# Decay matrix, plain casts and a new order of work in the opening of a fused retention and gated feed-forward kernel

## The chip, the core and the metric

The kernel runs on one core of a Trainium2 chip. The metric is the device time of one launch in microseconds (us), lower is better. It is given as the median of several runs. The profile shows one such execution.

[...] DMAs in this kernel are issued by SP and by POOL, and a few by ACT. All of them move data with the same 16 DMA engines. Each engine works through its own instructions in the order in which the program wrote them, and waits on semaphores for the others.

## The reference: what is computed

A recurrent attention with one decay per head (4 batches, 8 heads, 768 steps, head size 64) feeds a feed-forward block with a cosine gate (model size 512, inner size 2048).

```python
gamma = 1.0 - 2.0 ** (-5.0 - np.arange(H))
scale = 1.0 / np.sqrt(D)
for t in range(S):
    state = gamma[None, :, None, None] * state + np.einsum('bhd,bhe->bhde', k[:, :, t], v[:, :, t])
    y[:, :, t] = scale * np.einsum('bhd,bhde->bhe', q[:, :, t], state)
x = y.transpose(0, 2, 1, 3).reshape(B * S, H * D)
h = x @ w_in
out = (h * np.cos(h)) @ w_out
```

Inputs and outputs are float32. The kernel multiplies in bf16.

## The kernel before

**Tiles.** The 768 steps are cut into 6 chunks of 128. Two batches are handled together, so there are 12 "pairs" p = 0 to 11: chunk p mod 6 of batches 2·(p div 6) and the next one. The letter b (0 or 1) is the batch within the pair. A load of q, k or v for one pair and one b is a DMA of 256 KB. Two pairs make a group g of 512 tokens, for which the feed-forward part runs.

**The decay.** The factor gamma^(i-j) between step i and step j is split: q is multiplied by scale·gamma^i (table `gq`) and v by gamma^-j (table `gk`), so that the product of both gives the decay. The tables are made from `pos`, which POOL counts out (`iota`, L133), by eight small multiplications on DVE (L142) and two exponentials on ACT (L144, L145). The score matrix then needs only a mask of ones and zeros (`mask`).

**Stages of a pair.** `conv_q` (L156) and `conv_v` (L161) multiply by the tables and convert to bf16, `conv_k` (L166) only converts. `stage_t` (L173) transposes q and k on PE, eight small transposes for each b, and copies the PSUM bank out to `qkt` with ACT or DVE (L184, L186); from pair 4 on DMA transposes do this (`stage_t_dma`, L189). `stage_a` (L202) forms the scores of one b in two banks, one for each half j of the heads. `stage_m` (L214) multiplies each bank by the mask into `am`, on DVE. `stage_y` (L222) forms the output of both b from `am`, v and the state of the pairs before, copies it to `xt` on ACT (L240), then adds the pair's k and v to the state in PSUM (L248) and copies the state to `stb` (L253). `attend` is `stage_a` and `stage_m` for both b.

**The feed-forward part.** `pair_f` (L275) and `unit_f` (L267) multiply `xt` by `w_in` (L282, L270); `act` takes the cosine on ACT (L261) and the product on DVE (L265) into `gt`. `unit_o` (L291) multiplies `gt` by `w_out` (L296).

**What sets the order.** The order is written out by hand (`manual_schedule`), instruction by instruction, for all engines. PSUM banks are taken from and given back to a first-in first-out list of seven. `warm(n)` (L316) issues n matmuls on zeros, whose result is not used. The opening is the code from L325 to L355. In it the POOL queue holds loads of pair 0 and 1, the four `w_in` loads, `conv_v(1)`, three `w_out` loads and the loads of pairs 2 and 3; the SP queue holds five loads (L130, L131). After that the loop works through groups with the same stages in between.

Of the kernel before, what the change touches and what calls it, by code (L numbers as in the profile page):

```python
# [30 lines left out]
def kernel(  # L31
# [11 lines left out]
    C = 128  # L43
# [31 lines left out]
    sb([128, 1], FP32, "pad")  # L75
# [24 lines left out]
    gk = sb([128, NC, H], FP32, "gk")  # L100

# [29 lines left out]
    load(nc.sync, 1, ("q0", "v0"))  # L131
    load(nc.gpsimd, 0, ("k1",))
    nc.gpsimd.iota(pos, pattern=[[C, NC]], base=1, channel_multiplier=1,  # L133
                   allow_small_or_imprecise_dtypes=True)
    load(nc.gpsimd, 0, ("v0", "v1"))
    make_identity(nc, ident)
# [3 lines left out]
    nc.vector.memset(mask, 1.0)  # L140
    for h in range(H):
        nc.vector.tensor_scalar(out=lgp[:, :, h], in0=pos, scalar1=float(lg[h]),  # L142
                                scalar2=None, op0=ALU.mult)
# [3 lines left out]
    for t in stb:  # L147
        nc.vector.memset(t, 0.0)
    nc.gpsimd.affine_select(out=mask, in_=mask, compare_op=ALU.is_ge, fill=0.0,
                            base=0, pattern=[[1, 128]], channel_multiplier=-1)  # L150
# [5 lines left out]
    def conv_q(p, eng):  # L156
        for b in range(2):
            eng.tensor_tensor(out=qs[p % NB][:, b], in0=qf[SLOT[p]][b],  # L158
                              in1=bc(gq, p % NC), op=ALU.mult)
# [13 lines left out]
    def stage_t(p, split, fill=0):  # L173
        n = p % NB
        for b in range(2):
            if fill:
                warm(fill * b)
            bank = banks.take()
            tr = bank.bitcast(BF16).rearrange("p (w a t) -> p w a t", w=2, a=HP)
            for w, src in enumerate((qs[n], ks[n])):  # L180
                for a in range(HP):
                    nc.tensor.transpose(tr[:, w, a, :], src[:, b, 2 * a : 2 * a + 2, :], ident)  # L182
            if split is None or split and b == 1:
                nc.vector.tensor_copy(out=qkt[n][:, :, b], in_=tr)  # L184
            else:
                nc.scalar.copy(out=qkt[n][:, :, b], in_=tr)  # L186
            banks.give(bank)
# [26 lines left out]
    def stage_m(p, item):  # L214
        b, bk, ap = item
        for j in range(2):
            nc.vector.tensor_tensor(  # L217
                out=am[p % 2][b][j], in0=ap[j],
                in1=mask.unsqueeze(1).to_broadcast([128, HP, 128]), op=ALU.mult)
            banks.give(bk[j])  # L220

    def stage_y(p, copy_st=nc.vector.tensor_copy):  # L222
        c = p % NC
        n = p % NB
        for b in range(2):
            bank = banks.take()
            yp = bank.rearrange("p (a t) -> p a t", a=HP)
            for a in range(HP):
                if c > 0:
                    for j in range(2):  # L230
                        nc.tensor.matmul(  # L231
                            yp[ts(j, 64), a, :], lhsT=stb[p % 2][:, b, a, ts(j, 64)],
                            rhs=qt(n, b, a), start=True, stop=False,
                            skip_group_check=True)
                for j in range(2):
                    nc.tensor.matmul(  # L236
                        yp[ts(j, 64), a, :], lhsT=vs[n][:, b, 2 * a + j, :],
                        rhs=am[p % 2][b][j][:, a, :], start=(c == 0), stop=True,
                        skip_group_check=True)
            nc.scalar.copy(out=xt[(p // 2) % 2][:, :, ts(2 * (p % 2) + b, C)], in_=yp)  # L240
            banks.give(bank)
        if c == NC - 1:
            return
        for b in range(2):
            for a in range(HP):
                for j in range(2):
                    h = 2 * a + j
                    nc.tensor.matmul(  # L248
                        st_ps[ts(j, 64), b, a, :], lhsT=ks[n][:, b, h, :],
                        rhs=vs[n][:, b, h, :], start=(c == 0 and b == 0 and a == 0),  # L250
                        stop=True, skip_group_check=True)
        for j in range(2):
            copy_st(out=stb[(p + 1) % 2][ts(j, 64), :, :, ts(j, 64)], in_=st_ps[ts(j, 64)])  # L253

# [70 lines left out]
    load(nc.gpsimd, 1, ("k0", "q1", "k1", "v1"))  # L325
    for r in range(4):
        load_w_in(r)
    conv_v(1, nc.gpsimd)
    for r in range(3):
        load_w_out(r)  # L330
# [6 lines left out]
    conv_q(0, nc.vector)  # L337
    conv_k(0, True)
    conv_v(0, nc.vector)
    stage_t(0, False)  # L340
    warm(3)
    attend(0)
    conv_k(1, True)
    conv_q(1, nc.vector)
    warm(6)
    stage_y(0, nc.scalar.copy)
    warm(2)
    stage_t(1, None)
    attend(1)
    banks.give(spare)  # L350
    pair_f(0, 0, (0,))
    stage_y(1, nc.scalar.copy)
# [7 lines left out]
    for part in range(3):  # L360
        for j in range(4):
            unit_o(0, j, part)
            if part == 2 and j == 0:
                stage_t(2, None)
                conv_v(2, nc.vector)
            elif part == 2 and j == 1:
                stage_m(2, stage_a(2, 0))
            elif part == 2 and j == 3:
                stage_m(2, stage_a(2, 1))
# [12 lines left out]
    stage_t(3, None)  # L382
# [100 lines left out]
```

## Time and profile before

| | |
|---|---|
| median of 6 runs | 212.51 us (212.02 to 213.2) |
| time of the profiled execution | 212.39 us |
| its span, first to last instruction | 210.6 us |
| PE busy | 201.5 us, 96% |
| DVE, ACT, POOL busy | 116.1, 113.4, 84.3 us |
| first matmul of `w_in` (L282) | 16.68 us |
| second group of them, after the state of pair 1 (L282, 24 matmuls) | 19.48 us |
| HBM read, written | 27.26 MB, 6.29 MB |

The profiled execution spends 1.8 us outside its span. Times in a timeline count from the start of the span. A line of a timeline has a start, a duration, the engine, the source line, the operation, the tile written and the tiles read, and how many instructions are merged into it; in brackets stands how long the engine was idle before it and what it was waiting for. A line of the chain of waits has a start, a duration and the engine or DMA that the work passed through. In the view by stretches each row gives a start and an end, the length, and the busy time of every engine.

### The profile page before, as it was taken

How to read it: one execution, taken by the hardware profiler on the slowest of the kernel's cores; microseconds unless marked ns; L12 is line 12 of the kernel's file. 1: busy time of each engine (PE TensorE's matmuls, PEld its weight loads, DVE VectorE, ACT ScalarE, POOL GpSimd, SP SyncE). 2: the span in 40 equal slices, each digit the busy share in tenths (PEclk: the TensorE clock that was granted, in tenths of full speed). 3: DMA queues.
4: the chain of work that ended last, by engine and by line, in shares of the span. 5: the costliest groups of instructions: out<-in, count | busy, mean ns of one | idle time of the engine just before them, and what ended most of it. 6: DMA issues, size and time to landing. Idle time of an engine off the chain costs nothing.

```text
span 210.6 us, 4148 instructions
## 1 busy us (share of the span) xinstructions
PE 201.5 (96%) x1637; PEld 112.6 (53%) x1637; DVE 116.1 (55%) x187; ACT 113.4 (54%) x183; POOL 84.3 (40%) x98
## 2 busy tenths in 40 slices
PE   7678999999999999999999999999999999999992
PEld 2347654548998554555455455445545444444440
DVE  5496776281976755859585385484482333343000
ACT  5665884228799336656835745745545554553110
POOL 7995238499977907999352400000000000000000
PEclk9999999999999999999999999999999999999999
DMA  6999999999999999989998321321101101110121
GB/s 160 327 248 207 220 253 290 336 258 313 216 228 227 201 306 273 240 240 271 274 172 202 91 61 50 88 66 50 50 3 50 50 3 50 50 50 26 75 91 61
DMA packets 55844, 33.83 MB, mean 161 GB/s; under 512 B 47248, under 2 KB 49552, under 8 KB 55824
## 3 DMA queue, kind: packets, MB, share of 16 engines
q1 hardware_dynamic: 49472, 17.70, 36.9%
q0 software_dynamic: 6208, 15.73, 28.4%
q8 instruction: 13, 0.21, 0.4%
q10 hardware_dynamic: 144, 0.13, 0.2%
q14 instruction: 7, 0.06, 0.1%
HBM read 27.26 MB, written 6.29 MB: 159 GB/s over the span
## 4 chain that ended last, share of the span: by engine, by line
PE 88%; DVE 5%; DMA 3%; issue 1%; POOL 1%; ACT 0%; POOLq 0%; DVEq 0%
PE bank L296 39%; PE bank L270 32%; PE bank L282 8%; DMA vf<-in_v_dram 3%; PE bank L209 3%; PE bank L231 3%; PE bank L236 2%; DVE am L217 2%; DVE qs L158 1%; PE st_ps L248 1%; PE bank L182 1%; DVE qkt L184 1%; DVE vs L163 1%; POOL kf L112 0%; POOL vf L112 0%
## 5 line engine op out<-in xcount | busy, mean ns | idle before, releaser
L265 DVE TENSOR_TENSOR gt<-bank,cosb 128x512 bf16<-128x512 f32 x96 | 65.6, 690 | 63.5 <-ACT cosb L261 63.0
L261 ACT ACTIVATE cosb<-bank,halfpi 128x512 bf16<-128x512 f32 x96 | 65.5, 687 | 53.2 <-PE bank L270 46.8
L296 PE MATMUL bank<-w_out_sb,gt 128*128 128x512 bf16 x384 | 93.3, 379 | 0.0
L270 PE MATMUL bank<-xt,w_in 128*128 128x512 bf16 x304 | 75.1, 380 | 0.0
L296 PEld LDWEIGHTS <-gt 128*128 128x128 bf16 x384 | 36.7, 98 | 42.7
L270 PEld LDWEIGHTS <-w_in 128*128 128x128 bf16 x304 | 33.8, 114 | 30.8 <-issue 0.2
L217 DVE TENSOR_TENSOR am<-bank,mask 128x512 bf16<-128x512 f32 x48 | 30.2, 681 | 0.0
L158 POOL TENSOR_TENSOR qs<-qf,gq 128x512 bf16<-128x512 f32 x18 | 18.6, 1048 | 20.9 <-DMA qf<-in_q_dram 15.0
L308 ACT COPY ob<-bank 128x512 f32<-128x512 f32 x23 | 13.4, 587 | 23.0 <-PE bank L296 22.9
L112 POOL DMA_DIRECT2D kf<-in_k_dram x23 | 20.8, 907 | 4.5 <-DMA w_out_sb<-in_moe_w_out_dram 2.1
L163 POOL TENSOR_TENSOR vs<-vf,gk 128x512 bf16<-128x512 f32 x20 | 20.7, 1052 | 1.1 <-DMA vf<-in_v_dram 1.0
L282 PE MATMUL bank<-xt,w_in 128*128 128x256 bf16 x160 | 18.6, 273 | 0.0
L169 ACT CAST ks<-kf 128x512 bf16<-128x512 f32 x24 | 13.8, 614 | 8.3 <-DMA kf<-in_k_dram 8.3
L282 PEld LDWEIGHTS <-w_in 128*128 128x128 bf16 x160 | 17.1, 114 | 0.5
L112 POOL DMA_DIRECT2D vf<-in_v_dram x16 | 14.2, 889 | 4.2 <-DMA w_out_sb<-in_moe_w_out_dram 4.2
L240 ACT CAST xt<-bank 128x512 bf16<-128x512 f32 x24 | 13.0, 587 | 3.3 <-DVE gt L265 3.0
L236 PE MATMUL bank<-am,vs 128*64 128x128 bf16 x192 | 12.1, 219 | 0.9 <-DVE am L217 0.9
L236 PEld LDWEIGHTS <-vs 128*64 128x64 bf16 x192 | 10.1, 110 | 1.7 <-issue 1.7
L231 PEld LDWEIGHTS <-stb 128*64 128x64 bf16 x160 | 8.7, 109 | 4.3 <-issue 3.8
L231 PE MATMUL bank<-qkt,stb 128*64 128x128 bf16 x160 | 10.6, 222 | 0.0
L253 DVE CAST stb<-st_ps 64x512 bf16<-64x512 f32 x12 | 8.2, 687 | 3.5 <-PE st_ps L248 3.3
L209 PE MATMUL bank<-qkt 64*128 64x128 bf16 x192 | 8.2, 218 | 0.7 <-DVE qkt L184 0.4
(38 smaller groups left out, 70.0 us busy)
## 6 DMA issues: line engine op xcount, KB each, us to landing
kf<-in_k_dram POOLq DMA_DIRECT2D x23, 256.0 KB, 6.1
out_dram<-ob SPq DMA_DIRECT2D x23, 256.0 KB, 2.2
qf<-in_q_dram SPq DMA_DIRECT2D x19, 256.0 KB, 6.3
vf<-in_v_dram POOLq DMA_DIRECT2D x16, 256.0 KB, 6.7
vf<-in_v_dram SPq DMA_DIRECT2D x8, 256.0 KB, 5.8
w_in<-in_moe_w_in_dram POOLq DMA_DIRECT2D x4, 512.0 KB, 10.3
w_out_sb<-in_moe_w_out_dram POOLq DMA_DIRECT2D x4, 512.0 KB, 13.4
qf<-in_q_dram POOLq DMA_DIRECT2D x5, 256.0 KB, 6.9
```

What stands on the lines that cost most here:

```text
L112: eng.dma_start(out=t[SLOT[p]][b], in_=src[2 * bp + b, :, ds(c * C, C)].rearrange("h t d -> t h d"))
L158: eng.tensor_tensor(out=qs[p % NB][:, b], in0=qf[SLOT[p]][b], in1=bc(gq, p % NC), op=ALU.mult)
L163: eng.tensor_tensor(out=vs[p % NB][:, b], in0=vf[SLOT[p]][b], in1=bc(gk, p % NC), op=ALU.mult)
L209: nc.tensor.matmul(ap[j][:, a, :], lhsT=kt(n, b, a)[po : po + 64, :], rhs=qt(n, b, a)[po : po + 64, :], tile_position=(po, 0))
L217: nc.vector.tensor_tensor(out=am[p % 2][b][j], in0=ap[j], in1=mask.unsqueeze(1).to_broadcast([128, HP, 128]), op=ALU.mult)
L231: nc.tensor.matmul(yp[ts(j, 64), a, :], lhsT=stb[p % 2][:, b, a, ts(j, 64)], rhs=qt(n, b, a), start=True, stop=False, skip_group_check=True)
L236: nc.tensor.matmul(yp[ts(j, 64), a, :], lhsT=vs[n][:, b, 2 * a + j, :], rhs=am[p % 2][b][j][:, a, :], start=(c == 0), stop=True, skip_grou ...
L261: nc.scalar.activation(out=cb, in_=bank, func=AF.Sin, bias=halfpi)
L265: nc.vector.tensor_tensor(out=out, in0=bank, in1=cb, op=ALU.mult)
L270: nc.tensor.matmul(bank, lhsT=w_in_t(i, f), rhs=xt[g % 2][:, i, :], start=(i == 0), stop=(i == KIN - 1))
L282: nc.tensor.matmul(bank[:, ts(e, 256)], lhsT=w_in_t(i, f + e), rhs=xt[g % 2][:, i, ts(hf, 256)], start=(i == 0 and e == 0), stop=(i == KIN ...
L296: nc.tensor.matmul(bank, lhsT=gt[g % 2][:, f, ts(j, 128)], rhs=w_out_sb[:, f, :], start=(f == 0), stop=(f == KOUT - 1))
```

## The change

- `ident` and `mask` are made on DVE by comparing `rel`, a 128 x 128 table of column minus row, which POOL counts out. POOL's own building of both is gone. The eight multiplications for `lgp` become one, from eight one-column fills (`lgv`).
- ACT makes `decay`, eight 128 x 128 exponentials of `rel` (one for each head, zero above the diagonal). For pair 0 `stage_m` multiplies by `decay` in place of `mask`, so q, k and v of pair 0 are only cast: q and k on DVE, v on ACT into the new tile `vu`. v times `gk` is still made for the state, now on POOL.
- `stage_t` works on one b, and its copy out of PSUM is on DVE as a 32-bit `bitwise_or` with 0 (`copy_bits`). For pair 0 this copy was on ACT before, for pairs 1, 2 and 3 on DVE as a bf16 copy.
- The opening is reordered: the first half of the scores of b = 0 is masked before b = 1 is transposed, the second half after; `conv_q(1)` for b = 0 goes between them on DVE, for b = 1 behind the masks of pair 0. `stage_y` is cut into `half_y` and `stage_s`, and transposes of pair 1 go between the halves. There are 13 `warm` matmuls in place of 21.
- v of pair 1, b = 0, is loaded by POOL and no longer by SP. All loads of pair 1 by POOL stand ahead of anything else on that queue, `conv_v(0)` and `conv_v(1)` between the `w_in` loads.

```diff
     load(nc.sync, 0, ("q0", "k0", "q1"))
-    load(nc.sync, 1, ("q0", "v0"))
+    load(nc.sync, 1, ("q0",))
     load(nc.gpsimd, 0, ("k1",))
+    nc.gpsimd.iota(rel[:, 0], pattern=[[1, 128]], base=0, channel_multiplier=-1,
+                   allow_small_or_imprecise_dtypes=True)
     nc.gpsimd.iota(pos, pattern=[[C, NC]], base=1, channel_multiplier=1,
                    allow_small_or_imprecise_dtypes=True)
     load(nc.gpsimd, 0, ("v0", "v1"))
-    make_identity(nc, ident)
+    load(nc.gpsimd, 1, ("q1", "k0", "k1", "v0", "v1"))
...
-    nc.vector.memset(mask, 1.0)
     for h in range(H):
-        nc.vector.tensor_scalar(out=lgp[:, :, h], in0=pos, scalar1=float(lg[h]),
-                                scalar2=None, op0=ALU.mult)
+        nc.vector.memset(lgv[:, h : h + 1], lg[h])
+    for t in stb:
+        nc.vector.memset(t, 0.0)
+    nc.vector.tensor_scalar(out=ident, in0=rel[:, 0], scalar1=0.0, scalar2=None,
+                            op0=ALU.is_equal)
+    nc.vector.tensor_scalar(out=rel[:, 1], in0=rel[:, 0], scalar1=0.0, scalar2=1.0e6,
+                            op0=ALU.is_lt, op1=ALU.mult)
+    nc.vector.tensor_tensor(out=rel[:, 1], in0=rel[:, 1], in1=rel[:, 0], op=ALU.add)
+    nc.vector.tensor_scalar(out=mask, in0=rel[:, 0], scalar1=0.0, scalar2=None,
+                            op0=ALU.is_ge)
+    for h in range(H):
+        nc.scalar.activation(out=decay[:, h], in_=rel[:, 1], func=AF.Exp, bias=lnsc,
+                             scale=float(lg[h]))
+    nc.vector.tensor_tensor(out=lgp, in0=pos.unsqueeze(2).to_broadcast([128, NC, H]),
+                            in1=lgv.unsqueeze(1).to_broadcast([128, NC, H]), op=ALU.mult)
...
+    def copy_bits(out, bank):
+        nc.vector.tensor_scalar(out=out.bitcast(mybir.dt.uint32),
+                                in0=bank.bitcast(mybir.dt.uint32),
+                                scalar1=0, scalar2=None, op0=ALU.bitwise_or)
...
-            if split is None or split and b == 1:
-                nc.vector.tensor_copy(out=qkt[n][:, :, b], in_=tr)
-            else:
-                nc.scalar.copy(out=qkt[n][:, :, b], in_=tr)
-            banks.give(bank)
+        if on_act:
+            nc.scalar.copy(out=qkt[n][:, :, b], in_=tr)
+        else:
+            copy_bits(qkt[n][:, :, b], tr)
+        banks.give(bank)
...
+    def stage_m(p, item, parts=(0, 1)):
         b, bk, ap = item
-        for j in range(2):
-            nc.vector.tensor_tensor(
-                out=am[p % 2][b][j], in0=ap[j],
-                in1=mask.unsqueeze(1).to_broadcast([128, HP, 128]), op=ALU.mult)
+        for j in parts:
+            by = decay_j[:, j] if p == 0 else mask.unsqueeze(1).to_broadcast([128, HP, 128])
+            nc.vector.tensor_tensor(out=am[p % 2][b][j], in0=ap[j], in1=by, op=ALU.mult)
             banks.give(bk[j])
...
-    load(nc.gpsimd, 1, ("k0", "q1", "k1", "v1"))
-    for r in range(4):
-        load_w_in(r)
+    load_w_in(0)
+    conv_v(0, nc.gpsimd)
+    load_w_in(1)
     conv_v(1, nc.gpsimd)
+    load_w_in(2)
+    load_w_in(3)
...
     warm(10)
-    conv_q(0, nc.vector)
-    conv_k(0, True)
-    conv_v(0, nc.vector)
-    stage_t(0, False)
-    warm(3)
-    attend(0)
+    nc.vector.tensor_copy(out=qs[0][:, 0], in_=qf[0][0])
+    for b in range(2):
+        nc.vector.tensor_copy(out=ks[0][:, b], in_=kf[0][b])
+    stage_t(0, 0, False)
+    nc.vector.tensor_copy(out=qs[0][:, 1], in_=qf[0][1])
+    for b in range(2):
+        nc.scalar.copy(out=vu[:, b], in_=vf[0][b])
+    a00 = stage_a(0, 0)
+    stage_m(0, a00, (0,))
+    stage_t(0, 1, False)
+    conv_q(1, nc.vector, (0,))
+    stage_m(0, a00, (1,))
+    warm(1)
+    stage_m(0, stage_a(0, 1))
     conv_k(1, True)
-    conv_q(1, nc.vector)
-    warm(6)
-    stage_y(0, nc.scalar.copy)
+    conv_q(1, nc.vector, (1,))
     warm(2)
-    stage_t(1, None)
+    half_y(0, 0)
+    stage_t(1, 0, False)
+    half_y(0, 1)
+    stage_t(1, 1, False)
+    stage_s(0, nc.scalar.copy)
     attend(1)
     banks.give(spare)
+    half_y(1, 0)
     pair_f(0, 0, (0,))
-    stage_y(1, nc.scalar.copy)
+    half_y(1, 1)
+    stage_s(1, nc.scalar.copy)
     pair_f(0, 0, (1,))
     pair_f(1, 0)
```

## The prediction, made before the changed kernel was run

> **What bounds the kernel now.** First the page: its first section and, in the 40 slices of 5.3 us, the row of PE.
>
> ```profile
> PE 201.5 (96%) x1637; PEld 112.6 (53%) x1637; DVE 116.1 (55%) x187; ACT 113.4 (54%) x183; POOL 84.3 (40%) x98
> ...
> PE   7678999999999999999999999999999999999992
> ```
>
> PE is full from the fifth slice on; only the first four (21 us) have room. Its later work is unchanged in number, so the change is worth what it moves the moment from which PE runs without a gap: the 24 matmuls of L282 at 19.5 us. The chain of waits, in order of time, says what holds that moment:
>
> ```profile
> 3.50 5.78 DMA vf<-in_v_dram
> ...
> 9.90 2.48 DVE am L217 x4
> 12.38 2.52 DVE qs L158 x2
> ...
> 17.41 1.29 DVE am L217 x2
> ...
> 19.55 2.74 PE bank L282 x24
> 22.29 10.36 PE bank L270 x48
> ```
>
> A load of v (lands at 9.3), then DVE with hardly a pause until 18.70, then 0.8 us of PE (end of the output, state) and the dense part. The timeline of DVE shows the wait for v1 and its queue:
>
> ```profile
> 7.73 0.69 DVE L163 TENSOR_TENSOR vs<-vf,gk 128x512 bf16<-128x512 f32 x1
> 9.29 0.69 DVE L163 TENSOR_TENSOR vs<-vf,gk 128x512 bf16<-128x512 f32 x1 [0.87 <-DMA vf<-in_v_dram]
> 9.90 2.48 DVE L217 TENSOR_TENSOR am<-bank,mask 128x512 bf16<-128x512 f32 x4
> 12.30 2.59 DVE L158 TENSOR_TENSOR qs<-qf,gq 128x512 bf16<-128x512 f32 x2
> 14.82 1.48 DVE L184 COPY qkt<-bank 128x1024 bf16<-128x1024 bf16 x2
> 16.21 2.47 DVE L217 TENSOR_TENSOR am<-bank,mask 128x512 bf16<-128x512 f32 x4
> ```
>
> The masks stand behind v although they do not use it: the order on DVE makes them wait. The two q conversions take 2.59 us here; the same two at 34.01 us take 1.28. At 12.3 us POOL was converting v (11.79 to 12.88, 13.19 to 14.35), at 34 us it was only issuing DMAs.
>
> **When data arrive.** Issue times plus times to landing: q0 3.8, k0 4.7, k1 6.0, q1 6.9, v0 7.7, q0 of pair 1 8.6, v1 9.3; then v0, k0, q1, k1, v1 of pair 1 at 10.1, 10.8, 11.6, 12.4, 13.2: one load per 0.8 us. The `w_in` quarters land at 15.6, 17.8, 20.6 and 23.0. So the DMA engines are the limit, and a changed order only permutes the slots.
>
> **The change, part by part.** *SP and POOL queues.* SP has one load less, POOL one more, with the same total. POOL's order is now k1, v0, v1, then q1, k0, k1, v0, v1 of pair 1; after q0 of pair 1 (8.6) and v1 (9.3) I give these the slots 10.1, 10.9, 11.7, 12.5 and 13.2. Hence k1 of pair 1, for which ACT waits until 12.39 now, lands at about 11.7, and w_in keeps 15.6. POOL loses 0.94 us for `ident` and `mask` and gains a 128-wide iota (not in the trace; 0.16 for the 6-wide one, 0.43 for the select of this size: 0.3 taken). It issues to 10.0, makes v of pair 0 (2 x 1.05) to 12.1, issues w_in 1, makes v of pair 1 (landing 13.2) to about 15.1, and issues w_in 2 and 3 by 16.6; DMA reaches them only at 17.8. The w_out and pair 2 issues behind them slip by about 2 us; the first w_out part lands at 26.4 now and is used at 32.5.
>
> *Tables.* DVE's 0.86 us of L142 become eight fills (0.06 each by the lnsc row), four operations on 128 columns and one on 48, some 1.3 us, done by 3.9, when q0 lands. On ACT eight exponentials of 128: 0.33 for one of 48 columns, so 0.3 to 0.4 each, 2.5 to 3.2 us, from 3.6 to at most 6.8; needed at 7.7. Then gq, gk, the second table load (1.28), done by 8.8; v casts (0.62 each) at v0 and v1, done at 9.9; needed at 10.3. Hidden; 0.5 us more would still be.
>
> *Casts on DVE.* A float32 SBUF-to-SBUF cast is not in the trace. The nearest row, the two-input conversion, gives 0.69 as the upper end. [...] I take 0.42. [...]
>
> *The 32-bit copy.* [...] But the trace has 0.68 for 1024 bf16 elements (L184) and 0.68 for 512 float32 from the same banks (L217): the bf16 copy already moves two at a time. [...] For pairs 2 and 3 the copies were on DVE before, 1.29 for two, under a full PE: nothing. Against ACT's 1.01 (L186) DVE gains 0.3.
>
> *DVE in the new order*, with starts 0.62 apart in a run and 0.69 where one waits: cast of k1 from 6.05 to 6.5; copy b=0 to 7.2 (transposes done at 6.0); cast q1 to 7.5; mask 1 after its scores, 7.7 to 8.3; copy b=1 to 9.0; q0 of pair 1 to 9.6; three masks to 11.45; q1 of pair 1 to 12.1, or 12.9 if POOL's v conversion (to 12.1) delays it as in the 2.59 row; copies of pair 1 to 13.4 or 14.2; four masks, 2.5 us, to 16.0 or 16.8. Now it is 18.70. What falls out is v twice (1.4 us), the wait for v1 (0.87), a part of the q stretch and the wait before the copies.
>
> *PE around it.* Transposes of pair 1 need k (11.7 + 0.62, 12.3) and q (12.1 to 12.9): 13.4 at the latest. The state needs v x gk, 12.1. stb is ready on ACT at about 14.8, before the first half of the output (15.4). The first L282 group waits for w_in at 15.6 and ends at 16.6; the last half of the output and the state follow masks and this group, 0.8 us: **17.5** (17.4 to 17.7) against 19.48. The opening gains about 2.0 us. `w_in` parts 1, 2 and 3 are then needed at 20.1, 23.6 and 27 and land at 17.8, 20.6 and 23.0: no stall.
>
> *Is it kept?* The DMA row of the page reads 9 up to 85 us. K transposes of pair 5 are issued at 65.57 and land at 70.1, PE takes them at 72.35; of pair 7, 85.01, 91.4 and 92.19. If these landings stayed where they are, PE two us earlier would stall 1.2 us at pair 7. Their issue hangs partly on things that move too (ACT's output copies before the loads in the SP queue), so I charge a third: 0.4 us.
>
> **Sum:** 212.39 - 2.0 + 0.4 = 210.8 us, made against the profiled execution; the median of the runs is 0.12 above that. Its own range: 210.2 (all kept, no delay) to 211.4.
>
> **Rivals.**
> 1. *The DMA-bound middle takes most of it back.* Gain 2.0 - 1.2 = 0.8, perhaps less if POOL's 2 us later start of pair 2's loads runs on: 211.6 (to 212.2). For it: margins of 0.8 and 2.3 us. Against: no wait of PE for a DMA between 20 and 210 us.
> 2. *Slower: PE's clock falls.* With 13 fillers for 21, PE does little from 6 to 15 us. The ten first fillers are 0.43 us apart, those at 8.11 0.22: half speed until about 5 us, although the clock row says 1.00 throughout. If the clock drops back, nearly each of the 8-matmul steps on the path costs 0.4 more (about 2, so 0.9) and the dense part runs its first 4 us (as long as the warm-up at the start) at half, 2.0: +2.9 - 1.6 = +1.3, 213.7. [...] The row against it, by stretches:
>
> ```profile
> 6.50:8.10 1.60, 0.44 (x8) 0.45 (x9) 1.06 (x2) 1.06 (x2) 1.60 (x3) 1.00 1.14 321
> ```
>
> 0.44 of 1.60 busy, and still fast after it. New: groups of 0.4 to 0.6 at 5.3, 7.2, 7.6, 9.0, 9.5, 10.3, 12.3; no gap above 1.5 us. [...]
> [...]
>
> **Numbers.** No change means within 0.3%, 0.64 us: under 211.87 is faster. Main case 0.57, rival 1 0.18, rival 2 0.14, rival 3 0.11. Faster: main 0.56, 0.13 of rival 1, 0.03 of rival 3: 0.72. Same: 0.13. Slower: rival 2 and a little of 3, 0.15. The range runs from 209.9 (0.9 below, for copies that the 32-bit rule would shorten) to 212.6, over rivals 1 and 3; rival 2 stays out.
>
> **What would show it.** Last mask of pair 1 ending at 16 to 17 us; the 24-matmul group of L282 (now L306) near 17.5; casts of 0.4; copies of 0.68 as before; k of pair 1 at 11.7; PE idle under 0.5 us after 20 us. I am wrong if POOL's issues or the casts grow, if matmuls of 512 columns stand 0.43 apart after 6 us, or if PE waits for `qkt` at pairs 5 to 7.

## The result, and the profile after

The changed kernel took 210.75 to 217.95 us in 18 runs, with a median of 213.07; the kernel before took 212.52 (211.06 to 214.37) in the 39 runs beside it. Ratios here and below leave out executions more than 1.5% above the fastest of their kernel, nine of these 18, so the 0.9937 (95% interval 0.9911 to 0.9962) speaks for the better half of the changed kernel's executions alone. In that half the change gains 0.6%. Over all executions it gains nothing, and the reason is the subject of most of what follows: they form two groups. Of 19 executions with a recorded clock, eight have a granted PE clock of 0.996 or more; seven of these lie at 210.75 to 211.09, one at 211.95. The nine with a clock under 0.98 lie at 215.65 to 217.95. Two lie between (212.02 and 214.11, clocks 0.992 and 0.981).

The first profile of the changed kernel caught one of the second kind. From its page, the busy times (PE is the matrix engine, PEld its weight loads, DVE the vector engine, ACT the scalar engine, POOL the general engine; SP, which has no row there, is the queue processor) and the granted clock in slices of 5.3 us:

```profile
PE 204.7 (96%) x1629; PEld 114.9 (54%) x1629; DVE 117.4 (55%) x193; ACT 114.3 (53%) x189; POOL 87.8 (41%) x99
...
PEclk9855899999999999999999999999999999999999
```

The clock row was all nines in the profile before: here PE had half its speed in the third and fourth slice. A second profile (experiment `after_look` below) caught one of the first kind, 211.0 us:

```profile
PE 198.4 (95%) x1607; PEld 111.9 (53%) x1629; DVE 116.2 (56%) x193; ACT 114.2 (55%) x189; POOL 86.6 (41%) x99
...
PEclk9999999999999999999999999999999999999999
```

(22 matmul records are missing from this trace: 1607 matmuls against 1629 weight loads.) The view by stretches, cut where the 24 matmuls of `w_in` (now L306) begin, tells where the two executions differ. A row has start and end, length, then busy time and instructions of PE, PEld, DVE, ACT and POOL, the granted clock, the DMA share and GB/s. The slower execution:

```profile
0.00:22.87 22.87, 17.74 (x165) 10.39 (x165) 15.48 (x37) 11.68 (x24) 21.39 (x29) 0.70 1.02 223
22.87:213.90 191.03, 186.93 (x1470) 104.52 (x1464) 101.96 (x157) 102.58 (x166) 66.37 (x71) 1.00 0.62 150
```

The faster one:

```profile
0.00:18.02 18.02, 12.75 (x165) 7.48 (x166) 13.29 (x36) 11.43 (x24) 16.86 (x26) 1.00 1.01 240
18.02:209.20 191.18, 185.66 (x1448) 104.42 (x1464) 102.87 (x157) 102.79 (x167) 69.71 (x74) 1.00 0.63 154
```

The dense part is the same in all three: 191.03 and 191.18 us here, 191.12 (19.48 to 210.60) in the profile before. Nothing was lost or won behind the opening. The moment at which the dense part begins is everything: 19.48 before, 18.02 with the clock up, 22.87 with it down.

How the opening goes at its best, from the timeline of the 211.0 us execution (start, duration, engine, line, operation, tiles, count, in brackets the idle time before and its cause):

```profile
3.40 2.45 ACT L157 ACTIVATE decay<-rel,lnsc 128x128 f32<-128x128 f32 x8 [1.38 <-DVE rel L153]
...
3.83 0.89 DVE L363 CAST qs<-qf 128x512 bf16<-128x512 f32 x1 [0.20 <-DMA qf<-in_q_dram]
4.69 0.43 DVE L365 CAST ks<-kf 128x512 bf16<-128x512 f32 x1
6.32 0.43 DVE L365 CAST ks<-kf 128x512 bf16<-128x512 f32 x1 [1.20 <-DMA kf<-in_k_dram]
6.66 0.68 DVE L187 TENSOR_SCALAR qkt<-bank 128x512 uint32<-128x512 uint32 x1
7.26 0.42 DVE L367 CAST qs<-qf 128x512 bf16<-128x512 f32 x1
...
7.91 0.69 DVE L235 TENSOR_TENSOR am<-bank,decay 128x512 bf16<-128x512 f32 x1 [0.23 <-PE bank L224]
...
9.11 0.68 DVE L171 TENSOR_TENSOR qs<-qf,gq 128x512 bf16<-128x512 f32 x1
...
9.85 2.07 POOL L176 TENSOR_TENSOR vs<-vf,gk 128x512 bf16<-128x512 f32 x2
11.51 0.97 DVE L171 TENSOR_TENSOR qs<-qf,gq 128x512 bf16<-128x512 f32 x1
...
14.38 2.48 DVE L235 TENSOR_TENSOR am<-bank,mask 128x512 bf16<-128x512 f32 x4 [0.49 <-PE bank L224]
```

DVE has both casts of k done at 6.75, goes on without a wait for v, and its last mask ends at 16.86; before it was 18.70. How narrow this is, two lines show: the first q conversion ends at 9.79, and POOL begins its conversions of v at 9.85. The same steps in the profile of 215.65 us:

```profile
5.79 1.21 DVE L365 CAST ks<-kf 128x512 bf16<-128x512 f32 x2 [1.60 <-DMA kf<-in_k_dram]
...
7.77 1.22 DVE L367 CAST qs<-qf 128x512 bf16<-128x512 f32 x1
...
9.05 0.61 PE L197 MATMUL bank<-ident,qs 128*128 128x128 bf16 x4 [0.74 <-DVE qs L367]
...
10.73 1.13 DVE L171 TENSOR_TENSOR qs<-qf,gq 128x512 bf16<-128x512 f32 x1
...
13.58 1.58 DVE L171 TENSOR_TENSOR qs<-qf,gq 128x512 bf16<-128x512 f32 x1
...
17.68 2.48 DVE L235 TENSOR_TENSOR am<-bank,mask 128x512 bf16<-128x512 f32 x4 [0.70 <-PE bank L224]
...
19.86 1.89 PE L306 MATMUL bank<-xt,w_in 128*128 128x256 bf16 x8
```

Two things are longer, and neither is the work itself. The casts and the q conversions of DVE take up to 1.58 us where they took 0.42 and 0.68. And PE's groups take half as long again and more: four transposes 0.61 for 0.40, the eight matmuls of `w_in` 1.89 for 1.06. Side by side, starts in us:

| step | clock up | clock down | lag | what the lag grew by |
|---|---|---|---|---|
| first copy (L187) | 6.66 | 7.16 | 0.50 | k of b = 0 landed at 5.76 for 4.69 at the latest, and its cast took 0.89 for 0.43 |
| first mask | 7.91 | 8.92 | 1.01 | 0.51: cast of q, 1.22 for 0.42 |
| second copy | 8.52 | 10.12 | 1.60 | 0.59: 0.30 more of the late cast, 0.29 slow transposes |
| other masks of pair 0 | 9.71 | 11.78 | 2.07 | 0.47: q conversion, 1.13 for 0.68 |
| copies of pair 1 | 12.41 | 15.08 | 2.67 | 0.60: q conversion, 1.58 for 0.97 |
| masks of pair 1 | 14.38 | 17.68 | 3.30 | 0.63: transposes and scores at half clock |
| the 24 matmuls of `w_in` | 18.02 | 22.88 | 4.86 | 1.56: `w_in` group and the end of pair 1, slow |

So 2.4 of the 4.86 us stand beside long DVE instructions (0.5 of them beside a late load as well) and 2.5 beside PE's clock. That is a reading of two executions, not a proof; the experiments take each away in turn. The two are also not independent: the clock fell at 8.85 us, while PE stood idle behind the long cast of q (8.31 to 9.05).

### The profile page after: what moved, and what is told of

The parts are those of the page before. It is cut to its first block, busy times and chain, and to the rows that moved or that the text cites. A ratio compares the mean times of both kernels' runs of the same rounds, so it can differ in the third digit from the quotient of the medians.

```text
span 213.9 us, 4141 instructions
## 1 busy us (share of the span) xinstructions
PE 204.7 (96%) x1629; PEld 114.9 (54%) x1629; DVE 117.4 (55%) x193; ACT 114.3 (53%) x189; POOL 87.8 (41%) x99
## 4 chain that ended last, share of the span: by engine, by line
PE 89%; DVE 6%; DMA 2%; issue 1%; ACT 1%; SPq 0%; DVEq 0%; ACTq 0%
PE bank L320 39%; PE bank L294 31%; PE bank L306 8%; PE bank L224 3%; PE bank L246 3%; PE bank L251 3%; DMA kf<-in_k_dram 2%; DVE qkt L187 2%; PE bank L197 1%; DVE am L235 1%; DVE qs L171 1%; PE st_ps L267 1%; DVE qs L367 1%; DVE ks L365 0%; ACT cosb L285 0%
## 5 line engine op out<-in xcount | busy, mean ns | idle before, releaser
L235 DVE TENSOR_TENSOR am<-bank,mask 128x512 bf16<-128x512 f32 x44 | 27.8, 682 | 1.0 <-PE bank L224 0.9
L171 POOL TENSOR_TENSOR qs<-qf,gq 128x512 bf16<-128x512 f32 x18 | 18.5, 1047 | 21.7 <-DMA qf<-in_q_dram 21.7
L176 POOL TENSOR_TENSOR vs<-vf,gk 128x512 bf16<-128x512 f32 x22 | 23.4, 1087 | 1.2 <-DMA vf<-in_v_dram 1.2
L306 PE MATMUL bank<-xt,w_in 128*128 128x256 bf16 x160 | 19.4, 280 | 0.0
L306 PEld LDWEIGHTS <-w_in 128*128 128x128 bf16 x160 | 17.4, 115 | 1.0 <-issue 0.2
L115 POOL DMA_DIRECT2D vf<-in_v_dram x17 | 15.5, 913 | 5.3 <-DMA w_out_sb<-in_moe_w_out_dram 4.6
L182 ACT CAST ks<-kf 128x512 bf16<-128x512 f32 x22 | 12.6, 615 | 4.8 <-DMA kf<-in_k_dram 4.6
L246 PEld LDWEIGHTS <-stb 128*64 128x64 bf16 x160 | 9.2, 114 | 4.6 <-issue 4.2
L246 PE MATMUL bank<-qkt,stb 128*64 128x128 bf16 x160 | 11.4, 231 | 0.0
```

The costliest lines, as they stand in the source:

```text
L115: eng.dma_start(out=t[SLOT[p]][b], in_=src[2 * bp + b, :, ds(c * C, C)].rearrange("h t d -> t h d"))
L176: eng.tensor_tensor(out=vs[p % NB][:, b], in0=vf[SLOT[p]][b], in1=bc(gk, p % NC), op=ALU.mult)
L235: nc.vector.tensor_tensor(out=am[p % 2][b][j], in0=ap[j], in1=by, op=ALU.mult)
L246: nc.tensor.matmul(yp[ts(j, 64), a, :], lhsT=stb[p % 2][:, b, a, ts(j, 64)], rhs=qt(n, b, a), start=True, stop=False, skip_group_check=True)
L306: nc.tensor.matmul(bank[:, ts(e, 256)], lhsT=w_in_t(i, f + e), rhs=xt[g % 2][:, i, ts(hf, 256)], start=(i == 0 and e == 0), stop=(i == KIN ...
```

## The experiments

Two theories were open. **Clock:** 13 fillers for 21 leave PE too little to do, its clock falls, and the path pays. **Lock-out:** DVE instructions are held while POOL converts v or issues a DMA. The rows that suggest it are of the 215.65 us execution: the cast of q of 1.22 us (from 7.77) lay inside POOL's issues of v (7.47 to 9.47), and the q conversion of 1.58 us started at 13.58, 0.03 behind POOL's conversions (13.55 to 16.06). What holds DVE there, no trace shows. The rival to both was a load landing late.

### The changed kernel again

No edit. If the clock is the cause, there are two groups again, parted by the clock.

> The changed kernel as it is, once more. [...] Then single executions fall into two groups, one at 210.7 to 211.1 us with a granted clock above 0.99 and one at 214 to 218 us with 0.96 to 0.98, and no third cause is needed. Rival (a busy chip, nothing of the kernel): nearly all executions at 211 us here, or the kernel before has the same two groups beside it.

It took 211.05 to 217.22 us (six runs, clocks 0.966 to 1.0), ratio 0.9979 (0.9935 to 1.0023). In these runs the gain was not to be told from nothing. Nor was a third cause excluded: two of the six, at clocks of 1.0 and 0.994, took 212.11 and 212.57, above the better group. In its profile q of pair 1 landed at 11.3, for 9.2 in the 215.65 us execution, and every mask of DVE behind it waited: `L171` started at 11.36 after 1.31 us of idleness. So the landing varies too, and it may account for some of the scatter.

### Fillers alone

`warm` matmuls in the gaps of the opening, 29 for 13 (the 3 given to `stage_t` stand between the transposes of q and those of k):

```diff
-    stage_t(0, 0, False)
+    stage_t(0, 0, False, 3)
+    warm(2)
...
     a00 = stage_a(0, 0)
+    warm(3)
...
-    warm(1)
+    warm(2)
...
-    warm(2)
+    warm(3)
     half_y(0, 0)
+    warm(4)
...
     half_y(0, 1)
     stage_t(1, 1, False)
+    warm(2)
```

> The changed kernel with 29 filler matmuls in place of 13, the 16 more put where the matrix engine waits (between the q and k transposes of pair 0, behind its first score matrix, before the transposes of pair 1). Clock theory: granted clock 1.00 in every stretch after 6 us, all executions near 210.8 us (210.5 to 211.4), none above 212.5. Rival that the fillers stand in the way of the chain: about 0.2 us for each that runs past its gap, 211.5 to 212. Rival that the clock drops for another reason: still two groups.

215.48 us (212.33 to 215.82), ratio 1.0093 (1.003 to 1.0156): slower, at clocks of 0.99 to 0.998. A miss for the clock as the only cause. The timeline says what came first:

```profile
9.85 2.53 POOL L176 TENSOR_TENSOR vs<-vf,gk 128x512 bf16<-128x512 f32 x2
10.36 1.12 DVE L171 TENSOR_TENSOR qs<-qf,gq 128x512 bf16<-128x512 f32 x1 [0.58 <-DMA qf<-in_q_dram]
...
13.16 2.05 POOL L176 TENSOR_TENSOR vs<-vf,gk 128x512 bf16<-128x512 f32 x2
13.20 2.58 DVE L171 TENSOR_TENSOR qs<-qf,gq 128x512 bf16<-128x512 f32 x1
...
19.85 1.90 PE L308 MATMUL bank<-xt,w_in 128*128 128x256 bf16 x8
```

The second q conversion began 0.04 us behind POOL and ended at 15.78, 0.57 after both conversions of POOL (15.21): 2.58 us for a step of 0.69. It is not let in between them. In the first collision it was let in after one, and there POOL's pair took 2.53 for 2.05. The clock is not innocent in this execution either: it fell at 19.0, the eight matmuls of `w_in` took 1.90 for 1.06, and from the last mask (20.15) to the dense part (22.85) it was 2.70 us for 1.16.

### Fillers, and casts written with two inputs

The same, with the casts of pair 0 written as `max(x, x)`, a two-input operation:

```diff
-    nc.vector.tensor_copy(out=qs[0][:, 0], in_=qf[0][0])
+    nc.vector.tensor_tensor(out=qs[0][:, 0], in0=qf[0][0], in1=qf[0][0], op=ALU.max)
```

> As fill, but the four casts of q and k of pair 0 on the vector engine are written as the maximum of x with itself (two inputs, the same values). Lock theory (a one-input cast from SBUF and the general engine's issue of a DMA shut each other out): each of the four takes 0.63 to 0.70 us, none 0.9 or 1.2, the second q cast ends 0.5 us earlier than in fill, and the dense part starts 0.3 to 0.6 us earlier unless w_in holds it. Rival (the casts were late because their loads were): the q cast ends as in fill, at the same time to 0.2 us.

213.85 us (213.73 to 217.5), ratio 1.008 (1.0047 to 1.0114), clock 1.00 throughout the profile. The casts' four replacements took 0.68 to 0.69 each, one of them (7.29 to 7.97) fully inside POOL's issue of v (7.08 to 8.84). The casts of `fill` had taken 0.42 to 0.79, and one in the first profile 1.22. This fits a lock between POOL's DMA issues and the cast of 0.42 us alone, but one trace does not show it: over nine traces with casts, of the 30 casts listed singly, 20 kept 0.41 to 0.43 beside POOL's issues (all four in `nocol`) and ten took 0.50 to 1.22. Nor did the second q cast end 0.5 us earlier than in `fill`, where it had been free (7.97 for 7.74). The q conversions collided as before:

```profile
9.60 2.53 POOL L176 TENSOR_TENSOR vs<-vf,gk 128x512 bf16<-128x512 f32 x2
9.67 1.56 DVE L171 TENSOR_TENSOR qs<-qf,gq 128x512 bf16<-128x512 f32 x1
...
12.91 2.05 POOL L176 TENSOR_TENSOR vs<-vf,gk 128x512 bf16<-128x512 f32 x2
12.95 2.58 DVE L171 TENSOR_TENSOR qs<-qf,gq 128x512 bf16<-128x512 f32 x1
...
21.06 1.17 PE L308 MATMUL bank<-xt,w_in 128*128 128x256 bf16 x9
```

The two excesses, (1.56 - 0.69) + (2.58 - 0.69) = 2.76 us, taken from 21.06 give 18.3, close to where the 211.0 us execution starts its dense part (18.02). From the last mask (19.90) to there it is 1.16 us in both. With the clock at 1.00, lock-out alone accounts for the loss.

### Fewer fillers in the kernel before

The kernel before with the changed kernel's 13 fillers:

```diff
-    warm(3)
+    warm(1)
     attend(0)
     conv_k(1, True)
     conv_q(1, nc.vector)
-    warm(6)
-    stage_y(0, nc.scalar.copy)
     warm(2)
+    stage_y(0, nc.scalar.copy)
```

> The kernel before with 13 filler matmuls in place of 21 (1 for 3, 2 for 6, none for the last 2), nothing else. Clock theory: the clock drops here too in a part of the executions, and these stand 2 to 5 us above 212.5. Rival (the new order and not the number of fillers is at fault, or DMA and vector work in the opening): one group at 212.5, granted clock 0.998 in each.

212.48 us (211.66 to 213.16), ratio 1.0003 (0.9972 to 1.0035), clocks 0.974 to 0.991 in all six runs, where six of the eleven runs of the kernel before beside them had 0.996 or more. The clock did fall, as two stretches of its profile show, and the 2 to 5 us expected from it did not come:

```profile
8.00:10.00 2.00, 1.44 (x25) 0.96 (x23) 1.17 (x2) 1.01 (x1) 2.00 (x3) 0.77 1.10 320
10.00:12.00 2.00, 1.99 (x16) 0.66 (x11) 2.00 (x5) 0.62 (x1) 1.80 (x3) 0.50 1.11 361
```

Fewer fillers lower the clock, and here that costs little. In this profile the dense part starts at 20.70, 1.2 us later than in the first profile of the kernel before, but the six runs lie among those of the unedited kernel, whose clock also varies: of its 74 runs beside these experiments 29 with a clock of 0.996 or more had a median of 211.9, 36 at 0.986 to 0.995 of 212.6, and the nine below 213.9. So a low clock goes with one or two microseconds at most in the kernel before; in the changed kernel the runs below 0.98 lie 5 us above the others. That DVE's long queue covers part of PE's slow steps in the kernel before is likely, but not shown.

### No collision of POOL with DVE

POOL's conversions of v put behind all four `w_in` loads, `stage_s(0)` behind `attend(1)`:

```diff
-    load_w_in(0)
+    for r in range(4):
+        load_w_in(r)
     conv_v(0, nc.gpsimd)
-    load_w_in(1)
     conv_v(1, nc.gpsimd)
-    load_w_in(2)
-    load_w_in(3)
...
-    stage_s(0, nc.scalar.copy)
     attend(1)
     banks.give(spare)
+    stage_s(0, nc.scalar.copy)
```

> The changed kernel with the two v conversions of the general engine moved behind all four w_in loads (they start at about 12.5 us, not 10), and the state of pair 0 put behind the scores of pair 1. Collision theory: a two-input conversion on the vector engine that starts while the general engine converts v waits for it (1.1 to 2.6 us for 0.69). Here the first q conversion of pair 1 takes 0.69; the second too where it starts before 12.4. Then the dense part starts at 17.8 to 18.3 us and executions stand at 210.5 to 211.3 more often than in the changed kernel, median below 211.6. Rival (the clock is what makes executions slow): the same two groups, 210.9 and 214 to 218, as often as before.

217.16 us (214.92 to 219.98), ratio 1.0158 (1.0099 to 1.0218), clocks 0.960 to 0.976: all six in the slow group, where a median under 211.6 was expected. In its profile there was no collision, and still the dense part started at 21.84. Its timeline and a later stretch:

```profile
11.71 0.68 DVE L171 TENSOR_TENSOR qs<-qf,gq 128x512 bf16<-128x512 f32 x1
12.19 4.11 POOL L176 TENSOR_TENSOR vs<-vf,gk 128x512 bf16<-128x512 f32 x4
...
15.36 2.48 DVE L235 TENSOR_TENSOR am<-bank,mask 128x512 bf16<-128x512 f32 x4 [0.70 <-PE bank L224]
...
17.00 0.32 PE L246 MATMUL bank<-qkt,stb 128*64 128x128 bf16 x1 [0.67 <-ACT stb L272]
...
18.59 1.89 PE L306 MATMUL bank<-xt,w_in 128*128 128x256 bf16 x8
```

```profile
16.00:18.00 2.00, 1.04 (x22) 0.72 (x19) 1.84 (x4) 1.16 (x2) 2.00 (x5) 0.50 1.24 206
```

The masks end at 17.84, 0.98 behind those of the 211.0 us execution, and the dense part starts 3.82 behind. The end of pair 1 on PE is what grew, at a clock of 0.50. This is the counterpart to `fill_max`: there lock-out without the clock, here the clock without lock-out. The 3.82 are not the clock's alone, though: with `stage_s(0)` behind the scores of pair 1, PE waited 0.67 and 0.29 us for `stb`.

Two further forms were to make a collision less likely still. One had the first q conversion moved behind the masks of pair 0:

```diff
-    conv_q(1, nc.vector, (0,))
     stage_m(0, a00, (1,))
...
-    conv_q(1, nc.vector, (1,))
+    conv_q(1, nc.vector)
```

> As nocol, and the first q conversion of pair 1 is put behind the last mask of pair 0 instead of between the masks. Theory that masks stand behind the landing of q of pair 1 (seen at 8.6 to 11.3 us): with it out of the way the three masks end at 10.9 to 11.3 in every execution, and the spread is smaller than in nocol: all within 1.5 us, median 210.6 to 211.2. Rival (the landing does not matter, the converts come later now and meet the general engine's v): 0.5 to 1.5 us slower than nocol, q conversions of 1.1 to 2.6 us.

217.46 us (215.3 to 219.84), ratio 1.0185 (1.0131 to 1.0239), clocks 0.960 to 0.976: nothing gained. That the moved q conversions meet POOL's, as the rival of its expectation has it, the trace of the next kernel shows, which added 12 fillers to this one (the expectation counts 14):

> As nocol_late, with 27 filler matmuls in place of 13 in the waits of the matrix engine. If the clock costs time once collisions are gone: granted clock above 0.995 here against 0.96 to 0.99 in a part of nocol_late, and executions 0.5 to 3 us shorter than those. If the low clock was only a sign of a long opening (the kernel before with 13 fillers had 0.974 to 0.991 and the time of 21): no difference to nocol_late within 0.4 us.

219.03 us (212.75 to 220.68, twelve runs), ratio 1.0044 (1.0002 to 1.0085). Eight runs had a clock of 0.976 and took 218.4 to 220.7. A miss, and the worst collision of all:

```profile
11.98 4.55 POOL L176 TENSOR_TENSOR vs<-vf,gk 128x512 bf16<-128x512 f32 x4
12.09 5.00 DVE L171 TENSOR_TENSOR qs<-qf,gq 128x512 bf16<-128x512 f32 x2
```

The moved conversions ran right into POOL's four; 5.00 us for two (3.55 and 1.53), and PE stood still behind them. An order that only usually keeps two engines apart is not a protection.

### v of pair 0 on POOL in the kernel before

The part of the change that takes v off DVE, by itself:

```diff
     load(nc.gpsimd, 1, ("k0", "q1", "k1", "v1"))
+    conv_v(0, nc.gpsimd)
     for r in range(4):
         load_w_in(r)
...
-    conv_v(0, nc.vector)
```

> The kernel before with one part of the change alone: v of pair 0 is multiplied on the general engine, between its loads of pair 1 and w_in, and no longer on the vector engine. Theory that the gain of the change is v off the vector queue: masks of pair 0 start at 9.0 in place of 9.9, the q conversions behind them meet no v conversion, dense part at 17.5 to 18.5 against 19.5, time 210.5 to 211.6. Rival (plain casts, decay and half masks are needed for it): 212 to 213, since the output of pair 0 now waits for v from the general engine.

212.91 us (211.48 to 216.12), ratio 0.9997 (0.9953 to 1.004). Again two groups: six of the twelve runs, with clocks of 0.997 to 1.0, at 211.48 to 211.71, the others (0.981 to 0.992) at 214.1 to 216.1. The median of the six (211.61) is 0.3 us under the 211.95 of the unedited kernel's eight full-clock runs beside it, which spread from 211.18 to 212.36. So taking v off DVE is a small part of the gain at most, and it brings two groups along, with all 21 fillers in place. In its profile, one of the second kind:

```profile
8.10 3.34 DVE L158 TENSOR_TENSOR qs<-qf,gq 128x512 bf16<-128x512 f32 x1 [3.15 <-DMA qf<-in_q_dram]
8.83 2.05 POOL L163 TENSOR_TENSOR vs<-vf,gk 128x512 bf16<-128x512 f32 x2
...
11.49 0.61 PE L182 MATMUL bank<-ident,qs 128*128 128x128 bf16 x4 [5.02 <-DVE qs L158]
```

A q conversion, whose load landed at 8.1 (6.9 in the kernel before), took 3.34 us, up to 11.44, 0.56 behind the end of POOL's two conversions (10.88), and PE waited 5.02 us for it. The granted clock was 0.50 from 8 to 14 us and 1.00 again from 16. Here the low clock came with the wait and does not explain it: a run's mean clock alone does not tell cause from effect.

### The changed kernel at the full clock

> The changed kernel once more, one look, for the trace of an execution with the granted clock at 1.00. Theory (the gain is the shortened DVE queue, the clock and the meetings of DVE and POOL take it back): if the clock holds, span 209.0 to 209.3 us, the group of 24 matmuls of w_in starts at 18.0 to 18.3, both q conversions of pair 1 take 0.7 to 1.1 us, last masks end at 16.8 to 17.3. Otherwise span 212 to 214 and the group at 21 to 23. Rival (the difference lies later, in the DMA-bound middle): the group starts at the same moment and the rest of the span is longer than 191.1.

211.0 us, span 209.2; the lines are shown above. The theory's numbers held (dense part at 18.02, masks to 16.86), and the rival, a difference in the DMA-bound middle, falls: 191.18 us behind that point.

### A guard in place of luck

POOL is made to wait for a small table that DVE copies behind its second q conversion, so that POOL cannot start before:

```diff
-                              in1=bc(gk, p % NC), op=ALU.mult)
+                              in1=bc(gk2 if p < 2 else gk, p % NC), op=ALU.mult)
...
-    load_w_in(0)
-    conv_v(0, nc.gpsimd)
-    load_w_in(1)
-    conv_v(1, nc.gpsimd)
-    load_w_in(2)
-    load_w_in(3)
+    for r in range(4):
+        load_w_in(r)
...
     conv_q(1, nc.vector, (1,))
+    nc.vector.tensor_copy(out=gk2, in_=gk)
+    conv_v(0, nc.gpsimd)
+    conv_v(1, nc.gpsimd)
```

`stage_s(0)` stands behind `attend(1)` in it, as above.

> POOL's conversions of v read a copy of gk that DVE makes behind its second q conversion of pair 1, so they cannot meet the q conversions; the four w_in loads stand ahead of them on POOL. Theory (two causes, lock-out and clock): both q conversions 0.69, POOL's four conversions start at 12.2 to 12.5, last masks end at 16.3 to 17.0; where the clock is 1.00 the group of 24 matmuls starts at 17.7 to 18.3 and the run takes 210.5 to 211.2; where it falls, 213 to 216. Rival A (the lock-out alone): all runs at 210.5 to 211.3. Rival B (the clock alone): no better than the changed kernel, two groups of runs, ratio 1.00 to 1.01.

213.6 us (211.31 to 215.79, twelve runs), ratio 1.0015 (0.9972 to 1.0058). Both q conversions took 0.68; the clocks ran from 0.968 to 0.998, and with the lowest the time rose to 215.8. Rival B: with the q conversions free, the slow runs stay, though spread from 211.3 to 215.8 and no longer in two groups. The casts were not guarded (the cast of q took 0.83 in its profile).

The same with fillers (the 16 of `fill` and four behind `stage_s(0)`, 20 more; the expectation counts 21):

> As the run with the guarded conversions, with 21 more filler matmuls in the gaps of PE between 5 and 15 us. Theory (two causes, lock-out and clock, both now met): clock 0.99 or more in every run, both q conversions 0.69, all runs at 210.5 to 211.5, ratio 0.990 to 0.996. Rival (the fillers themselves delay the path, as each holds PE 0.22 us): clock 1.00 but 211.5 to 212.5. Second rival (a third cause, the landing of the loads by SP): 211 to 214 with the clock at 1.00, and a q conversion that waits for its DMA in the trace.

212.46 us (211.91 to 213.46), ratio 0.9998 (0.997 to 1.0026). The second group is gone: all twelve clocks at 0.996 or more and no run over 213.5. The gain is gone too. The masks ended at 17.51, but the dense part began only at 19.25, 1.74 later, where the changed kernel at its best needs 1.16. The trace shows one cost of this order:

```profile
15.63 1.19 ACT L275 CAST stb<-st_ps 64x512 bf16<-64x512 f32 x2 [1.75 <-PE st_ps L270]
```

The state of pair 0 comes behind the scores of pair 1 here, and behind POOL's guarded conversions (those of pair 0 end at 15.08). So `stb` is copied by 16.82 (14.76 at the changed kernel's best), and the output of pair 1 waits for it. What the fillers cost was not tried alone. Against `guard`, which has the same order, they alone made the difference: this is the experiment that shows the clock as a cause.

### Two guards

The changed kernel's order kept, with one guard in front of each pair's conversion and 13 more fillers:

```diff
     conv_q(1, nc.vector, (0,))
+    nc.vector.tensor_copy(out=gk2, in_=gk)
+    conv_v(0, nc.gpsimd)
+    load_w_in(1)
...
     conv_q(1, nc.vector, (1,))
+    nc.vector.tensor_copy(out=gk3, in_=gk)
+    conv_v(1, nc.gpsimd)
+    load_w_in(2)
+    load_w_in(3)
```

> The changed kernel's order with two guards and 13 more filler matmuls: POOL's conversions of v of pair 0 read a copy of gk that DVE makes behind its first q conversion of pair 1, those of pair 1 one that it makes behind the second; w_in part 1 stays between them. Theory (two causes; the guarded run with more fillers was late because all four conversions of v came after the second q conversion and its fillers stood in front of transposes): first q conversion 0.69, second 0.69 to 1.1, POOL's conversions of pair 1 end at 14.5 to 15.0 and not at 17.1, last masks end at 16.8 to 17.2, group of 24 matmuls at 18.0 to 18.5, clock 0.99 or more in every run, median 210.9 to 211.5, ratio 0.992 to 0.996. Rival (13 fillers are too few for the clock): runs at 213 to 216 with the clock under 0.98 among them. Second rival (fillers on the path are what costs): clock 1.00 and 212 to 212.5, with gaps of DVE in front of its copies that end with PE.

211.7 us (211.1 to 212.79, twelve runs), ratio 0.9969 (0.9948 to 0.9989), twelve clocks of 0.996 or more. The gain of 0.3% is half of what the better group of the changed kernel has, but it counts all twelve runs. The profiled execution was the slowest of the twelve (212.79 us): q of pair 1 landed late, as the first line shows, and both the guard and the masks waited for it.

```profile
10.94 0.69 DVE L173 TENSOR_TENSOR qs<-qf,gq 128x512 bf16<-128x512 f32 x1 [1.06 <-DMA qf<-in_q_dram]
11.55 0.18 DVE L369 COPY gk<-gk 128x48 f32<-128x48 f32 x1
...
11.82 2.05 POOL L178 TENSOR_TENSOR vs<-vf,gk 128x512 bf16<-128x512 f32 x2 [2.02 <-DVE gk L369]
13.44 0.97 DVE L173 TENSOR_TENSOR qs<-qf,gq 128x512 bf16<-128x512 f32 x1
```

The second q conversion still met POOL's first pair (11.82 to 13.87) and took 0.97: the guard parts it from the second pair only. What is left of the scatter, 211.1 to 212.8, goes with the landing in this one trace; no run fixed the landing, so this stays argued. Five kernels together:

| kernel | fillers | guard | runs with clock 0.996 or more | median, all runs | the kernel before, beside it |
|---|---|---|---|---|---|
| changed | 13 | no | 8 of 19 | 213.07 | 212.52 |
| `fill` | 29 | no | 1 of 6 | 215.48 | 212.35 |
| `guard` | 13 | yes | 2 of 12 | 213.60 | 212.69 |
| `guard_fill` | 33 | yes | 12 of 12 | 212.46 | 212.69 |
| `guard_two` | 26 | yes | 12 of 12 | 211.70 | 212.43 |

With fillers alone or the guard alone there are runs of 215 us and more; with both there is none over 213.5 in 24. Of these two, `guard_two` is the one whose interval lies wholly below 1. It does not reach the changed kernel's best: 211.1 against 210.75. The order of `guard_two` was not run without its guards or without its extra fillers, so how its gain divides between them is argued from `guard`, `guard_fill` and the traces.

## Why the prediction was right, and where it was not

The forecast was 210.8 us, and the changed kernel takes 210.75 to 211.1 where its clock holds. The way there was the predicted one: DVE's queue ended earlier, and the dense part began earlier by 1.46 us. But the two sides of the sum were off by 0.5 and 0.3 us in opposite directions, so the closeness of the number is in part luck. And the forecast holds for the better group alone: the median over all 18 executions, 213.07, lies above the stated range (209.9 to 212.6), and a rival that was given 0.14 is a part of what the other executions show.

**The bound.** Right. The dense part is 191.0 to 191.2 us in all three profiles, and the time follows the moment at which it starts. The chain of waits no longer begins with a load of v but with one of k; its end, at the full clock:

```profile
9.11 0.68 DVE qs L171
9.79 1.80 DVE am L235 x3
11.59 0.90 DVE qs L171
...
16.27 1.00 PE bank L306 x8
17.27 0.18 PE bank L246 x2
...
17.84 0.25 PE st_ps L267 x16
```

**Tables.** Right, hidden. The eight exponentials took 2.45 us, to 5.85, and ACT waited for v (7.93) after the second table load. The 128-wide count on POOL was 0.26, taken as 0.3.

**The casts.** The 0.42 came true (0.42 and 0.43 where free), but when it was put into the sum no row of the kernel before showed it: the nearest, the two-input conversion, has 0.69. The sum has no term for a cast held by POOL, and that was right only in some executions: at the full clock one of four casts took 0.89, off the path; in the first profile the cast of q took 1.22, and 0.51 us of path went with it. Of the 30 casts counted above ten took 0.50 or more beside POOL's issues, 20 did not.

**The 32-bit copy.** Right: 0.68 and 0.69, as the bf16 copy. The 0.9 us by which the stated range reaches lower for a shorter copy, no run shows: the eight copies of this form in the first profile took 0.68 to 0.69.

**DVE in the new order.** The last mask ended at 16.86, against "16.0 or 16.8". The allowance for one collision, 0.8, was 0.29 in this execution (0.97 for 0.68) and 0.9 or 1.9 in others. The first q conversion, for which none was allowed, escaped by 0.06 us here and took 1.12 and 1.56 in `fill` and `fill_max`. The smaller collision was offset by a later start: k1 landed at 6.3 for 6.0, and the masks of pair 0 ended at 11.59 for 11.45.

**PE around it.** The term that was mis-sized: 0.8 us from the last mask to the dense part took 1.16 (16.86 to 18.02). The prediction let the first `w_in` group wait for `w_in` "at 15.6" and end at 16.6. It started at 16.21, held by half of the output of pair 1, whose mask came at 15.68, and ended at 17.27, 0.41 behind the last mask. The opening gained 1.46 us, not 2.0.

**Is it kept?** The charge of 0.4 for the DMA-bound middle was not there: 191.18 against 191.12, and no wait of PE for a DMA in its view of waits. The stalls feared at pairs 5 and 7 did not come. The landings of `w_in` parts 1 to 3 were misread: they were 19.1, 21.5 and 24.0 before, not 17.8, 20.6 and 23.0 (12.9 us from issue to landing for the last, issued at 11.04). They still came before they were needed. In the sum, -1.46 + 0.06 = -1.40 against the predicted -1.6: two errors of opposite sign, one of 0.5 and one of 0.3.

**The rivals.** Rival 1 (the middle) is out by these numbers. Rival 3, given 0.11, had DVE's queue stay as long as it was; it is out where the clock holds, 16.86 for 18.70. In the 215.65 us execution the last mask did not end before 20.16, and the cast of q, 1.22 for 0.42 beside POOL's issues, is a part of that. Rival 2 (PE's clock) came true in about half of the runs, though not as it was worked out. The stretch shown against it, PE busy for 0.44 of 1.60 us and still fast, was of one execution that stayed lucky. Its price of +2.9 is near the 2.5 us that stand beside the clock in the table above, by luck: 2.0 of it were for a dense part that starts at half clock, and the dense part did not (191.03 us, clock 1.00); the whole 2.5 lie in the opening, where it had put 0.9. What it lacked besides is the lock-out, about as much again. What makes the clock drop, these two executions do not tell. The length of a gap did not decide: the clock dropped at 8.85 us in the first profile, where the longest wait of PE since 5 us had been 0.90 us, and it held in the 211.0 us execution, where PE waited 1.73 us (up to 7.40). Nor did a busy share decide: from 4 to 8 us PE was busy for 2.31 us there and for 2.27 where the clock held to the end. Which of the two a given execution does, no run here explains.

## What to carry to other kernels

A shortened queue is worth what its own trace says only if the instructions in it keep their length: when work is moved to POOL, look for every DVE instruction that can meet it and grow (here the q conversions, 0.68 free and up to 3.55 beside POOL's conversions, and the casts, 0.42 free and up to 1.22 beside its DMA issues), and make the meeting impossible with a dependence rather than unlikely with an order. When filler work on PE is taken out, compare the granted clock over many executions, not in one profile, since the same kernel keeps it in one and loses it in the next. And a change that is faster at its best can be no faster at its median; the distribution over runs belongs to the result.

## What was not expected of the hardware

- DVE is not always let in after one instruction of POOL: with 0.69 us of its own it took 1.56 behind one conversion of POOL, 2.58 behind two and 3.55 behind three.
- In one trace a q conversion started 0.73 us ahead of POOL's conversion and still waited for both (8.10 to 11.44; POOL 8.83 to 10.88). Why, is open: POOL was issuing a DMA when it started (7.93 to 8.81).
- A lower clock left the median of the kernel before where it was (212.48 for 212.35, six runs at 0.974 to 0.991; in the profiled one, 213.16 us, PE ran at half clock from 9 to 19 us).
- The same cast beside POOL's DMA issues took 0.41 to 0.43 in 20 of the 30 places counted above and 0.50 to 1.22 in the others. Written as `max(x, x)` it took 0.69 in all four places of one trace; whether that form is safe, one trace does not show.
